# First product of two tiles by seven block products instead of eight, in rounds that take first and second product by turns

## The chip, the cores and the metric

The kernel runs on one core of one Trainium2 chip. The metric is device time in microseconds, the median of several executions. The core has four engines that compute, each with a queue of its own that it works through in order: TensorE (PE in the profile, with PEld for its weight loads), VectorE (DVE), ScalarE (ACT) and GpSimd (POOL). SyncE (SP) starts most transfers. [...]

## The reference

Attention with a threshold, then a feed-forward block. All arrays are float32 (the weights may come as 64-bit floats).

```python
batch, n_heads, seq, head_dim = (8, 8, 576, 64)
scores = q @ k.T / 8
scores = where(scores >= max(scores) - tau, scores, -1e9)
attn = exp(scores - max(scores)); attn /= sum(attn) + 1e-9
x = (attn @ v) laid out as (8 * 576, 512)         # 4608 tokens
h = x @ w_in                                      # (4608, 1024)
solu = h * softmax(h)
ln = (solu - mean) / sqrt(var + 1e-6) * g_ln
out = ln @ w_out                                  # (4608, 512)
```

## The kernel before

Attention goes by slots. A slot `(b, kind, hp, r)` holds 128 query rows of two heads against all 576 keys; a batch has 18 slots (`PER`), the kernel 144 (`NS`). The main loop runs in rounds, one slot each, and writes out by hand what every engine does in which order (`tc.manual_schedule()`); what is issued earlier in a round stands earlier in its engine's queue. A round issues, in this order:

- `begin` jobs, then `ff_norm` of a tile;
- `scores` (line 472): eight matmuls of 64x64 blocks into the two PSUM tiles `s0` and `s1`, of which there is one each, so the next round's scores wait until they are read;
- `maxes` on DVE (line 494, a scan of each head's scores that leaves the row's extreme), `ramp` on ACT (line 509, reads the scores and the extreme), `exps` on ACT (line 518, in place with row sums);
- `normalise` of the slot before on POOL (lines 525 to 528), then `middle` jobs;
- one `step` of the feed-forward block, and, where it is due, `attend_steps` (line 582, the product pv of the transposed weights `wT` with v, three rounds after its second slot) with `attended` (line 614), ACT's copy of pv into the token tile `xh` or `xe`;
- `blocks` of the slot before: two transposes on DVE (line 540); after every second slot the transposed rows are sent by SP into `wT` (lines 549 to 556);
- `late` jobs; GpSimd's scaling and gathering of coming q; a `flip` on DVE (line 212) for coming q or k; loads.

The feed-forward block works on 36 tiles of 128 tokens: 32 from `xh` (two tiles for each batch and kind), four from `xe`. Each tile takes four steps in four rounds: two halves of the first product (`ff_h`, line 647, 16 matmuls of 64x64x512 each; line 637 with whole 128x128 blocks after the last slot) and two halves of the second (`ff_o`, line 752). So two rounds with `ff_h`, and mostly pv, are followed by two with `ff_o`. Between the products stand, in jobs of later rounds: `ff_max` (DVE, 662), `ff_exp` (ACT, 671), `ff_mul` (DVE, 677), `ff_sum` (POOL, 682 and 683), `ff_stats` (DVE 692 and 693, then five small operations on POOL), `ff_norm` (ACT, 713, writes `V`), `ff_norm2` (DVE, 718, in place on `u`), `ff_swap` (four transfers from `u` into `V`), `ff_turn` (DVE, 739, writes `uT`). `ff_out` (ACT, 767) and `ff_store` end a tile.

In `ff_h` the two row halves of PE write different banks and change over between the two halves of the product; a `fence`, a memset on POOL that waits for the last matmuls, stands between (line 108). PSUM tiles for `ff_h`, `ff_o` and pv come from two tags (`p0`, `p1`) that `take` hands out and the reader gives back.

## Time and profile before

| | us |
|---|---|
| median of 3 runs | 860.36 |
| fastest, slowest | 860.07, 865.73 |
| the profiled execution | 864.95 |
| its span | 863.2 |
| PE busy (share of the span) | 817.0 (95%) |
| DVE busy | 673.5 (78%) |
| ACT busy | 572.1 (66%) |
| POOL busy | 495.1 (57%) |
| all `ff_o` matmuls, line 752 | 273.1 |
| all split `ff_h` matmuls, line 647 | 246.1 |

The span runs from the first to the last instruction of one profiled execution; the device time has 1.75 us more around it. Busy times of a group count every stretch in which one of its instructions runs; matmuls overlap their neighbours, so the groups of PE sum to more than PE's own busy time. In the profile's groups, `out<-in` names tiles, `xN` counts instructions, and one float32 matmul shows as two.

### The profile page before, as it was taken

Reading aid. Unit: us, or ns where it says so; the run is one execution under the profiler, and the core shown is the slowest. Engines: PE = TensorE matmul, PEld = TensorE weight load, DVE = VectorE, ACT = ScalarE, POOL = GpSimd, SP = SyncE. Lnnn points to the kernel's source line nnn. Section 1 sums busy time; section 2 is a strip of 40 time slices with the busy share of each in tenths; the row PEclk is TensorE's granted clock in tenths of the full one; section 3 lists DMA queues with packets and bytes.
Section 4 is the critical chain, followed back from the end, with each engine's and each line's share of the span. In section 5 each row is a group of like instructions: output and inputs, shape, how many; then the busy total and the mean of one; then the engine's idle time right before and its main releaser. Section 6 shows DMA issues by size and latency. Waiting matters only on the chain.

```text
span 863.2 us, 36114 instructions
## 1 busy us (share of the span) xinstructions
PE 817.0 (95%) x15361; PEld 634.7 (74%) x15361; DVE 673.5 (78%) x1232; ACT 572.1 (66%) x1153; POOL 495.1 (57%) x936
## 2 busy tenths in 40 slices
PE   4659789999999999999999999999999999999997
PEld 3437567777688888888788886777788888887655
DVE  4987777978788888888788887888888888787361
ACT  5876867777667767777677766767677776775121
POOL 2876756566666656565656655565666655555120
PEclk9878999999999999999999999999999999999999
DMA  9999796997878778888788787888788887555312
GB/s 288 243 254 251 185 203 162 234 248 196 224 196 219 202 196 208 220 214 198 201 202 222 198 194 192 212 222 206 183 228 229 193 196 186 154 141 140 69 38 62
DMA packets 83712, 168.54 MB, mean 195 GB/s; under 512 B 15448, under 2 KB 45152, under 8 KB 83552
## 3 DMA queue, kind: packets, MB, share of 16 engines
q1 hardware_dynamic: 82416, 164.25, 75.5%
q8 instruction: 120, 1.97, 1.0%
q10 hardware_dynamic: 1136, 2.00, 0.7%
q14 instruction: 40, 0.33, 0.1%
HBM read 46.14 MB, written 9.44 MB: 64 GB/s over the span
## 4 chain that ended last, share of the span: by engine, by line
PE 84%; DMA 6%; ACT 4%; issue 2%; DVE 2%; POOL 1%; SPq 1%; ACTq 0%; DVEq 0%
PE o_ps L752 26%; PE h_ps L647 23%; PE s_ps L472 16%; PE pv L582 15%; DMA wT<-T 4%; PE h_ps L637 3%; ACT w L509 1%; ACT w L518 1%; DMA qT<-flip 1%; DMA w<-w 1%; DVE w L494 1%; DMA k<-in_k_dram 1%; ACT qT L374 0%; PE s_ps L337 0%; POOL w L528 0%
## 5 line engine op out<-in xcount | busy, mean ns | idle before, releaser
L752 PE MATMUL o_ps<-w,uT 64*64 64x256 f32 x4608 | 273.1, 376 | 4.3 <-issue 1.9
L494 DVE CUSTOM_DVE_ANT_0 w<-s_ps,tau_t 128x576 f32<-128x576 f32 x280 | 200.0, 751 | 94.4 <-PE s_ps L472 67.0
L509 ACT ACTIVATE w<-s_ps,nth 128x576 f32<-128x576 f32 x280 | 197.0, 739 | 110.8 <-DVE nth L494 90.8
L752 PEld LDWEIGHTS o_ps<-w,uT 64*64 64x64 f32 x4608 | 221.5, 133 | 59.3 <-ACT xh L614 12.0
L528 POOL TENSOR_SCALAR w<-w,sm 128x576 f32<-128x576 f32 x288 | 221.5, 781 | 14.3
L540 DVE STREAM_TRANSPOSE T<-w 128x576 f32<-128x576 f32 x288 | 207.5, 755 | 22.0 <-POOL w L528 20.6
L647 PE MATMUL h_ps<-w,xh 64*64 64x512 f32 x1856 | 223.1, 589 | 0.7 <-issue 0.7
L518 ACT ACTIVATE w<-w,ntau 128x576 f32<-128x576 f32 x288 | 219.8, 768 | 0.0
L582 PEld LDWEIGHTS pv<-wT,v 64*64 64x64 f32 x5760 | 179.7, 137 | 37.4 <-issue 12.8
L472 PE MATMUL s_ps<-kT,qT 64*64 64x512 f32 (+1 forms) x2048 | 177.1, 413 | 14.0 <-ACT w L509 12.0
L582 PE MATMUL pv<-wT,v 64*64 64x128 f32 (+1 forms) x5760 | 179.5, 266 | 9.7 <-DMA wT<-T 7.2
L647 PEld LDWEIGHTS h_ps<-w,xh 64*64 64x64 f32 x1856 | 131.7, 133 | 65.4 <-issue 10.6
L525 POOL TENSOR_SCALAR sm<-sm 128x2 f32<-128x2 f32 x144 | 34.7, 241 | 203.7 <-ACT w L518 200.1
L526 POOL TENSOR_TENSOR sm<-sm,mone 128x2 f32<-128x2 f32 x144 | 105.8, 735 | 12.0
L472 PEld LDWEIGHTS s_ps<-kT,qT 64*64 64x64 f32 x2048 | 76.0, 136 | 21.1 <-ACT w L509 16.4
L614 ACT COPY xh<-pv 128x256 f32<-128x256 f32 x64 | 25.0, 390 | 83.3 <-PE pv L582 83.2
L713 ACT ACTIVATE V<-u,nb,rs 128x1024 f32<-128x1024 f32 x36 | 44.7, 1241 | 39.6 <-POOL nb L703 32.6
L739 DVE STREAM_TRANSPOSE uT<-V 128x1024 f32<-128x1024 f32 x36 | 44.3, 1230 | 15.2 <-DMA V<-u 14.8
L518 ACT ACTIVATION_READ_ACCUMULATOR w<-w,ntau 128x1 f32 x288 | 55.9, 194 | 0.0
L677 DVE TENSOR_TENSOR u<-h_ps,u 128x1024 f32<-128x1024 f32 x36 | 42.8, 1189 | 9.7 <-ACT u L671 9.7
L718 DVE TENSOR_SCALAR u<-u,rs,nb 128x1024 f32<-128x1024 f32 x36 | 35.5, 987 | 17.2 <-ACT V L713 17.1
L662 DVE TENSOR_REDUCE hm<-h_ps 128x1 f32<-128x1024 f32 x36 | 43.0, 1193 | 6.0 <-PE h_ps L647 3.3
(88 smaller groups left out, 562.9 us busy)
## 6 DMA issues: line engine op xcount, KB each, us to landing
wT<-T SPq DMA_DIRECT2D x160, 288.0 KB, 6.2
wT<-T SPq DMA_DIRECT2D x64, 576.0 KB, 5.5
V<-u SPq DMA_DIRECT2D x144, 64.0 KB, 3.4
out_dram<-ob SPq DMA_DIRECT2D x71, 128.0 KB, 2.5
q<-in_q_dram SPq DMA_DIRECT2D x24, 288.0 KB, 6.1
qT<-flip SPq DMA_DIRECT2D x48, 144.0 KB, 3.8
k<-in_k_dram SPq DMA_DIRECT2D x24, 288.0 KB, 5.9
kT<-flip SPq DMA_DIRECT2D x48, 144.0 KB, 4.2
```

The lines of the kernel that those rows point to most:

```text
L472: nc.tensor.matmul(out=ps[h][ROWS[y], ks], lhsT=lhsT, rhs=d["kT"][ROWS[h], ks], start=True, stop=True,)
L494: nc.vector.tensor_tensor_reduce(out=w, in0=ps[:, 0:S], in1=(zero if loose else tau_t).to_broadcast([P, S]), scale=1.0, scalar=BIG, op0=AL ...
L509: nc.scalar.activation(out=d["w"][x], in_=d["w"][x] if d["loose"] else d["ps"][x][:, 0:S], func=AF.Prelu, bias=d["nth"][x], scale=-1.0, al ...
L518: nc.scalar.activation(out=w, in_=w, func=AF.Exp, bias=ntau, scale=1.0, accum_out=sm[:, x : x + 1])
L526: nc.gpsimd.tensor_tensor(out=sm, in0=sm, in1=mone, op=ALU.pow)
L528: nc.gpsimd.tensor_scalar(out=w, in0=w, scalar1=sm[:, x : x + 1], scalar2=1.0, op0=ALU.mult, op1=ALU.mult)
L540: nc.vector.transpose(out=T[:, :, r, h, :], in_=w)
L582: nc.tensor.matmul(out=to, lhsT=d["v"][ROWS[u], (h0 + h - u) % 4 if b > 1 else h0 + h, m ^ 4 * u if m < 8 and b < 2 else m,], rhs=rhs, sta ...
L647: mm = nc.tensor.matmul(out=h[ROWS[y], f], lhsT=x[ROWS[r], c, ROWS[y]], rhs=w1_parts[ROWS[r], c, part ^ r], start=part == 0 and c == 0, st ...
L713: nc.scalar.activation(out=V, in_=u, func=AF.Identity, bias=nb, scale=rs)
L739: nc.vector.transpose(out=uT, in_=d["V"].rearrange("p y (m x) -> p m y x", x=32))
L752: nc.tensor.matmul(out=d["o"][ROWS[z], 512 * (r ^ other) : 512 * (r ^ other) + 256], lhsT=d["uT"][ROWS[r], m].rearrange("p y x -> p (y x)" ...
```

## The change

From round 30 (`START`) to the end:

- Two PSUM tiles are taken for good: `both["h"]` (two banks) for the first product, and `both["o"]`, which holds pv in columns 0 to 127 and the second product in columns 256 to 511 of each of its two banks.
- Even rounds take first product and pv, odd rounds half of a second product (`steady_round`).
- Two tiles of one batch and kind form a pair. Their first product, which has eight block products (2 tiles x 2 halves of the contraction x 2 halves of the columns), is made of seven, with sums and differences of blocks in the manner of Strassen and Winograd. Sums of the weights are made once, on GpSimd in rounds 21 to 28 (`seven_weights`); sums of the tokens per pair, on GpSimd (`sums_a`, `sums_b`). A pair takes seven phases of eight matmuls in four even rounds: two, two, two and one. Partial results are read out in between by ACT (`keep_half`) and added up by DVE, which keeps a running maximum (`add_half`).
- pv accumulates onto zeros, which DVE writes after ACT's copy (`clear`).
- `ff_norm2` goes to GpSimd.
- `xe` tiles keep eight block products (`one_h`), in two even rounds each.
- There are two token tiles `xh` where there were four, three tiles `u`, and one `ob`. q and k of the first two batches are loaded by pairs of heads (`load_pair`) where they came by four heads.

The eight rounds from a pair's first phase on are numbered r to r+7 in `new_pair`. The core of the diff:

```diff
         b, kind, hp = key
         unit = units[key]
         wT = unit["wT"]
-        unit["y"] = take("pv")
+        unit["y"] = (None, both["o"]) if "o" in both else take("pv")
         _, y = unit["y"]
         y = y.rearrange("p (u n) -> p u n", u=2)
                                 m ^ 4 * u if m < 8 and b < 2 else m,
                             ],
                             rhs=rhs,
-                            start=m == 0, stop=m == NK - 1,
+                            start=m == 0 and "o" not in both, stop=m == NK - 1,
+                            skip_group_check="o" in both,
                         )
...
-                    [P, NP, 256], F32, tag=f"xh{(2 * b + kind) % 4}", bufs=1, name="xh"
+                    [P, NP, 256], F32, tag=f"xh{kind}", bufs=1, name="xh"
...
         nc.scalar.copy(out=to, in_=y)
-        pairs_free.append(tag)
...
+        if tag:
+            pairs_free.append(tag)
+        else:
+            clear()
+    def clear():
+        nc.vector.memset(both["o"].rearrange("p (u n) -> p u n", u=2)[:, :, 0:P], 0.0)
+    both = {}
+    seven = {}
+    order_u = []
+    def new_u():
+        x = len(order_u) % 3 if "h" in both else 0
+        if "h" in both:
+            order_u.append(x)
+        return work.tile([P, DFF], F32, tag=f"u{x}", bufs=1, name="u")
+    def block(i, j, c):
+        return w1_parts[:, 2 * i + c, j]
...
+    def seven_weights(n):
+        what, c = divmod(n, 2)
+        if what < 3:
+            if n < 3:
+                to = raw_tile("k")[:, 0:512]
+            elif n < 5:
+                to = const_sums[n - 3]
+            else:
+                to = work.tile([P, 512], F32, tag="obT", bufs=1, name="sums")
+            seven[what, c] = to.rearrange("p (a x) -> p a x", x=32)
+        to, a, b, op = (
+            lambda: (seven[0, c], block(0, 1, c), block(0, 0, c), ALU.subtract),
+            lambda: (seven[1, c], block(1, 1, c), seven[0, c], ALU.subtract),
+            lambda: (seven[2, c], block(1, 0, c), seven[1, c], ALU.subtract),
+            lambda: (block(0, 1, c), block(0, 1, c), block(1, 1, c), ALU.subtract),
+        )[what]()
+        nc.gpsimd.tensor_tensor(out=to, in0=a, in1=b, op=op)
+    def sums_a(ts):
+        x1, x2 = [tokens(t) for t in ts]
+        both["s"] = work.tile([P, 2, P], F32, tag="sum", bufs=1, name="sum")
+        nc.gpsimd.tensor_tensor(out=both["s"], in0=x2[:, 0:2], in1=x2[:, 2:4], op=ALU.add)
+        nc.gpsimd.tensor_tensor(out=x2[:, 0:2], in0=x2[:, 0:2], in1=x1[:, 0:2], op=ALU.subtract)
+    def sums_b(ts):
+        x1 = tokens(ts[0])
+        nc.gpsimd.tensor_tensor(out=x1[:, 0:2], in0=both["s"], in1=x1[:, 0:2], op=ALU.subtract)
+        nc.gpsimd.tensor_tensor(out=x1[:, 2:4], in0=x1[:, 2:4], in1=x1[:, 0:2], op=ALU.subtract)
...
+    PHASES = ((1, 2), (2, 1), (6, 5), (5, 6), (7, 3), (3, 7), (4, 4))
+    def product(ts, n, c):
+        x1, x2 = [tokens(t) for t in ts]
+        return {
+            1: lambda: (x1[:, c], block(0, 0, c)),
+            2: lambda: (x1[:, 2 + c], block(1, 0, c)),
+            3: lambda: (x1[:, 2 + c], block(1, 1, c)),
+            4: lambda: (x2[:, 2 + c], seven[2, c]),
+            5: lambda: (both["s"][:, c], seven[0, c]),
+            6: lambda: (x1[:, c], seven[1, c]),
+            7: lambda: (x2[:, c], block(0, 1, c)),
+        }[n]()
+    def phase(ts, k):
+        h = both["h"]
+        last = []
+        for c in range(2):
+            for r, n in enumerate(PHASES[k]):
+                bank = r if n == 4 else n in (2, 3, 5)
+                x, w = product(ts, n, c)
+                for y in range(2):
+                    mm = nc.tensor.matmul(
+                        out=h[ROWS[y], 512 * bank : 512 * bank + 512],
+                        lhsT=x[ROWS[r], ROWS[y]], rhs=w[ROWS[r]],
+                        start=c == 0 and (n, r, k) in ((1, 0, 0), (2, 1, 0), (5, 1, 2), (4, 1, 6)),
+                        stop=c == 1 and k in (1, 3, 5, 6), skip_group_check=True,
+                    )
+                    if k in (1, 3, 5) and not last:
+                        sync(mm, both["fence"])
+                    last.append(mm)
+        if k in (0, 2, 4):
+            both["fence"] = fence(last[-4:])
...
+    def keep_half(t, g, bank):
+        nc.scalar.copy(out=half(ffn[t]["x"], g), in_=half(both["h"], bank))
+    def add_half(t, g, bank):
+        d = ffn[t]
+        m = small.tile([P, 1], F32, tag=f"hm{g}", name="hm")
+        d["m"].append(m)
+        to = half(d["x"], g)
+        nc.vector.tensor_tensor_reduce(
+            out=to, in0=half(both["h"], bank), in1=to, scale=1.0, scalar=-BIG,
+            op0=ALU.add, op1=ALU.max, accum_out=m,
+        )
...
+    def pair_exp(t):
+        d = ffn[t]
...
+        nc.vector.tensor_scalar(
+            out=nm, in0=m, scalar1=n, scalar2=-1.0, op0=ALU.max, op1=ALU.mult
+        )
+        d["u"] = new_u()
+        d["se"] = small.tile([P, 1], F32, tag="se", name="se")
+        nc.scalar.activation(
+            out=d["u"], in_=d["x"], func=AF.Exp, bias=nm, scale=1.0, accum_out=d["se"]
...
+    def pair_mul(t):
+        d = ffn[t]
+        nc.vector.tensor_tensor(out=d["u"], in0=d["x"], in1=d["u"], op=ALU.mult)
+    def new_pair(ts, r):
+        a, b = ts
+        def at(when, n, job):
+            when.setdefault(r + n, []).append(job)
+        def first():
+            for t in ts:
+                ffn[t] = dict(m=[])
+            ffn[a]["x"] = new_u()
+            keep_half(a, 0, 0)
+            add_half(a, 0, 1)
+            sums_b(ts)
+        def second():
+            ffn[b]["x"] = new_u()
+            keep_half(a, 1, 0)
+            keep_half(b, 1, 1)
+        at(late, 1, first)
+        at(late, 3, second)
+        at(late, 5, lambda: (add_half(a, 1, 1), add_half(b, 1, 0), pair_exp(a)))
+        at(late, 6, lambda: (pair_mul(a), ff_sum(a)))
+        at(middle, 7, lambda: ff_stats(a))
+        at(late, 7, lambda: (keep_half(b, 0, 1), add_half(b, 0, 0), pair_exp(b)))
+        at(begin, 8, lambda: ff_norm(a))
+        at(middle, 8, lambda: (ff_norm2(a), ff_swap(a)))
+        at(late, 8, lambda: (pair_mul(b), ff_sum(b)))
+        at(middle, 9, lambda: ff_stats(b))
+        at(late, 9, lambda: ff_turn(a, r + 9))
+        at(begin, 10, lambda: ff_norm(b))
+        at(middle, 10, lambda: (ff_norm2(b), ff_swap(b)))
+        at(late, 14 if r + 14 <= NS else 11, lambda: ff_turn(b, rnd))
+        oq.extend(ts)
...
-        nc.vector.tensor_scalar(
+        (nc.gpsimd if "h" in both else nc.vector).tensor_scalar(
             out=d["u"], in0=d["u"], scalar1=rs, scalar2=nb, op0=ALU.mult, op1=ALU.add
...
-    def ff_o(t, part):
+    def ff_o(t, ms):
         d = ffn[t]
-        other = len(t) == 3 and t[0] > 1 and t[2]
-        if part == 0:
-            d["otag"], d["o"] = take("o_ps")
-        for m in range(NC * part, NC * part + NC):
+        if ms.start == 0:
+            if "o" in both and rnd < NS:
+                d["otag"], d["o"], d["oat"] = None, both["o"], 256
+            else:
+                (d["otag"], d["o"]), d["oat"] = take("o_ps"), 0
+        for m in range(ms.start, ms.stop):
             for r in range(2):
                 for z in range(2):
+                    of = 512 * r + d["oat"]
                     nc.tensor.matmul(
-                        out=d["o"][ROWS[z], 512 * (r ^ other) : 512 * (r ^ other) + 256],
+                        out=d["o"][ROWS[z], of : of + 256],
                         lhsT=d["uT"][ROWS[r], m].rearrange("p y x -> p (y x)"),
...
-        d["ob"] = ob = work.tile([P, DM], F32, tag="ob", name="ob")
-        ob, o = [x.rearrange("p (r n) -> p r n", r=2) for x in (ob, d["o"])]
+        d["ob"] = ob = work.tile([P, DM], F32, tag="ob", bufs=1, name="ob")
+        ob = ob.rearrange("p (r n) -> p r n", r=2)
+        o = d["o"].rearrange("p (r n) -> p r n", r=2)[:, :, d["oat"] : d["oat"] + 256]
+        if len(t) == 3 and t[0] > 1 and t[2]:
+            o = o[:, ::-1]
...
-        (15, load_one, 1, "k"),
-        (16, load_one, 1, "q"),
+        (10, load_pair, 4, "k"),
+        (10, load_pair, 5, "k"),
+        (11, load_pair, 4, "q"),
+        (11, load_pair, 5, "q"),
+        (15, load_pair, 6, "k"),
+        (15, load_pair, 7, "k"),
+        (16, load_pair, 6, "q"),
+        (16, load_pair, 7, "q"),
         (17, load_v, 0, (0,)),
...
-        load_qk(0, 0)
+        load_pair(0, "q")
+        load_pair(1, "q")
+        load_pair(0, "k", nc.scalar)
+        load_pair(1, "k")
...
-        load_qk(0, 1)
+        load_pair(2, "q")
+        load_pair(2, "k")
...
+        def steady_round(due):
+            if (rnd - START) % 2:
+                o_steps(NC)
+                return
+            if not hsteps and ready and ready[0][0] <= rnd:
+                ts = ready.pop(0)[1]
+                if len(ts) == 2:
+                    new_pair(ts, rnd)
+                    sums_a(ts)
+                    for k in range(0, 7, 2):
+                        hsteps.append([lambda k=k, ts=ts: phase(ts, k)])
+                        if k < 6:
+                            hsteps[-1].append(lambda k=k, ts=ts: phase(ts, k + 1))
+                else:
+                    new_one(ts[0], rnd)
+                    sum_one(ts[0])
+                    hsteps.append([lambda t=ts[0]: None, lambda t=ts[0]: one_h(t, 0)])
+                    hsteps.append([lambda t=ts[0]: one_h(t, 1)])
+            steps = hsteps.pop(0) if hsteps else []
+            if steps[1:] or steps and rnd >= NS:
+                steps[0]()
+            if due:
+                key = pv_due.pop(0)[1]
+                for _ in attend_steps(key):
+                    pass
+                done_with(key)
+            elif rnd >= NS:
+                o_steps(NC // 2 if steps else NC)
+            if steps and rnd < NS or steps[1:]:
+                steps[-1]()
...
+            if rnd == START:
+                both["h"], both["o"] = take("h2")[1], take("ov")[1]
+                clear()
+                oq.append(prev)
+                prev = None
+                assert cur is None and quarter == 0
...
+                cur is None and quarter == 0 and ready and ready[0][0] <= rnd < START - 2
...
+                    load_pair(3, "k")
+                    load_pair(3, "q")
...
-            if quarter < 2 and cur is not None:
+            if rnd >= START:
+                steady_round(due)
...
+            if 21 <= rnd < 29:
+                seven_weights(rnd - 21)
```

## Prediction

> **What bounds the kernel now.** First the page's head: TensorE (PE) is busy 95% of the span, VectorE (DVE) 78%.
>
> ```profile
> span 863.2 us, 36114 instructions
> PE 817.0 (95%) x15361; PEld 634.7 (74%) x15361; DVE 673.5 (78%) x1232; ACT 572.1 (66%) x1153; POOL 495.1 (57%) x936
> ```
>
> Then the timeline of PE in the steady part (start us, length us, engine, line, operation).
>
> ```profile
> 401.13 1.21 PE L472 MATMUL s_ps<-kT,qT 64*64 64x64 f32 x11
> 402.01 3.77 PE L647 MATMUL h_ps<-w,xh 64*64 64x512 f32 x32
> 405.44 2.19 PE L582 MATMUL pv<-wT,v 64*64 64x128 f32 x71
> ...
> 407.50 1.21 PE L472 MATMUL s_ps<-kT,qT 64*64 64x64 f32 x11
> 408.38 3.79 PE L752 MATMUL o_ps<-w,uT 64*64 64x256 f32 x64
> 411.83 1.31 PE L472 MATMUL s_ps<-kT,qT 64*64 64x64 f32 x16
> 412.81 3.79 PE L752 MATMUL o_ps<-w,uT 64*64 64x256 f32 x64
> ```
>
> Groups follow with no gap, so I count start to start. A round with half of a first product takes 6.37 us (scores 0.88, product 3.43, pv 2.06), a round with half of a second product 4.43 (0.98 and 3.45); two and two make 21.6 per four rounds, 43.2 per eight. PE sets the pace here. How near the others are shows in one round that starts at 674.98, on all engines:
>
> ```profile
> 674.98 1.29 PE L472 MATMUL s_ps<-kT,qT 64*64 64x64 f32 x16
> 676.47 0.72 DVE L494 CUSTOM_DVE_ANT_0 w<-s_ps,tau_t 128x576 f32<-128x576 f32 x1
> ...
> 677.12 0.76 DVE L494 CUSTOM_DVE_ANT_0 w<-s_ps,tau_t 128x576 f32<-128x576 f32 x1
> 677.30 1.42 ACT L509 ACTIVATE w<-s_ps,nth 128x576 f32<-128x576 f32 x2 [1.55 <-DVE nth L494]
> ...
> 679.24 1.38 DVE L540 STREAM_TRANSPOSE T<-w 128x576 f32<-128x576 f32 x2
> ...
> 679.37 0.77 ACT L518 ACTIVATE w<-w,ntau 128x576 f32<-128x576 f32 x1
> ...
> 680.13 0.57 ACT L767 COPY ob<-o_ps 128x512 f32<-128x512 f32 x1
> ```
>
> From it: the first scan (L494) starts 1.4 us after the scores do (1.49 here); two scans take 1.38 of DVE; the ramps (L509) start 0.83 after the first scan and end at 2.25; ACT is through the exponentials (L518) at 3.66; the two transposes (L540) take 1.40. The next scores need the ramps done (they free the banks s0, s1), so an odd round of 4.43 us lets the scan be late by about 0.7 (4.43 less 1.4, 2.25 and a hand-off), an even one of 6.37 by about 2.7.
>
> **The change, part by part.** Fewer products: 14 pairs of tiles take 56 matmuls where they took 64. Eight matmuls are a quarter of the pair's eight-round share, 3.43/2 = 1.715 us, so 14 x 1.715 = 24.0 us less on PE; a cycle of eight rounds (call them e0 o1 e2 o3 e4 o5 e6 o7) takes PE 43.2 - 1.7 = 41.5, e6 holding one phase only (4.65 us). In the tail four tiles at 7.0 us (L637) become two at 6.0 and others at 6.9; its PE work is 66.3 us against 69.5.
>
> Moved between engines, per pair. From DVE go two maxima (L662, 1.19 each) and two second normalisations (L718, 0.99). To DVE come four `add_half` (the form of L494 at 512 columns: 0.61, with its read 0.65), two `hm` (0.15 to 0.41, taken 0.20) and a memset of the pv columns after each of four pv. The trace has no such memset; between the 128x64 copy (0.21) and the 128x256 copy (0.42), I take 0.35. DVE's work rises by about 0.7 us, to some 36 of 41.5. To ACT come four copies of 512 columns (L767, 0.57). To GpSimd come two normalisations (L528's 1.36 ns per column x 1024 = 1.39; bounds 0.99 by DVE's row, 2.56 by L312's 2.5 ns) and four sums of 256 columns (L312: 0.64). Its queue then holds 35 us of the cycle, counting 2.6 per round for lines 525 to 528.
>
> ```profile
> L528 POOL TENSOR_SCALAR w<-w,sm 128x576 f32<-128x576 f32 x288 | 221.5, 781 | 14.3
> L677 DVE TENSOR_TENSOR u<-h_ps,u 128x1024 f32<-128x1024 f32 x36 | 42.8, 1189 | 9.7 <-ACT u L671 9.7
> L302 DVE SCALAR_TENSOR_TENSOR em<-em 128x512 int32<-128x512 int32 x16 | 13.7, 856 | 0.0
> L312 POOL TENSOR_TENSOR w<-w,em 128x512 int32<-128x512 int32 x16 | 20.5, 1279 | 0.0
> ```
>
> **The added wait.** pv now lands in a tile that is never released, and `clear()` zeroes it. In DVE's queue the memset stands behind the scans and *ahead of the transposes*, and it waits for ACT's pv copy, which stands behind that round's ramps and exponentials. From the first scan: exponentials done 3.66, copy (L614) 0.40, two hand-offs of 0.08 (the scan's read ends at 677.21, the ramp starts at 677.30), memset 0.35, so 4.5 to 4.6; transposes to 5.9. Before, 2.8 sufficed: about 3 us of DVE lie idle in each even round. Queued behind are the transposes, the multiplications, the turns and the next scan; the next odd round's second product also waits for the memset. With the next scan due 6.37 after this one there is 0.4 us of room, and none in e0 and e6.
>
> Walk of one steady cycle, first scan to first scan:
> - e0: ACT still owes the copy, exponential and first normalisation (0.57, 1.30, 1.24) from o7, so the ramps start 1.1 late; 5.9 + 1.1 + multiplication of tile b 1.13 = 8.1.
> - o1: scans 1.38, statistics 1.45, transposes 1.40, turn 1.15, `add_half` 0.65, `flip` 0.70 = 6.7.
> - e2: `sums_b` stands in GpSimd's queue behind the chain of b's statistics (2.83 + 1.94 + 1.28 = 6.1 after o1's scan), so phase 2 starts 2.5 late on PE: 6.3.
> - o3: PE's own 4.43.
> - e4: phase 4 must wait until ACT, behind o3's exponentials, has copied both banks (3.66 + 2 x 0.57 + 0.08 = 4.9 after o3's scan; PE is there at 3.9): 6.37 + 0.9 = 7.3.
> - o5: 1.38 + 1.40 + 2 x 0.65 + 0.20 + 0.70 = 5.0.
> - e6: ramps 0.4 late behind tile a's exponential; 5.9 + 0.4 + turn 1.15 + multiplication 1.13 = 8.6, where PE has only 4.65 to do.
> - o7: 1.38 + 1.45 + 1.40 + 0.1 + 0.65 + 0.20 + 0.70 = 5.9.
>
> Sum 52.3 us, against 43.2 before and 41.5 of PE.
>
> **The sum.** Rounds 30 to 143 take 613.7 us before (scores at 175.06 to the tail at 788.78). After: 12 cycles (627.6), six rounds of the thirteenth (52.3 - 8.6 - 5.9 = 37.8), three stretches of four rounds for the `xe` tiles at half a cycle each (78.4): 744, less 8 (the first cycle has no predecessor whose statistics, turn and multiplication, 3.7, fall into it; the last 17 rounds have no `flip`, 6 x 0.7): 736, so +122. Rounds 0 to 29: loads in other pieces and eight GpSimd subtractions (1.28 each, in rounds where GpSimd is 61% busy), taken as 0 (-3 to +3). Tail: -3 if nothing waits, +10 if the last tiles' chain lies open; taken as 0. Span 863 + 122 = 985, with the 1.75 us around it 987. The profiled execution (864.95) lies 0.53% above the median of the three (860.36); so the forecast for the median is 982 us.
>
> The multiplication now has both inputs in SBUF. L302, of that kind, takes 1.67 ns per column, L677 1.16: 1.13 to 1.71 us. At the upper end two per cycle add 1.2, or about 16 us over the 13 cycles. [...]
>
> **Rivals.**
> A, faster: PE stays the bound and every new wait is covered. For it: DVE's plain work, 36 us, fits in 41.5. Against: the idle 3 us in four rounds do not fit beside it (36 + 12 = 48). Time: 863.2 - 24.8 (24.0 and 0.8 in the tail) = 838.4; for the median 836.
> B, slower by a ring alone: the transposes of one even round feed the pv of the next (two rounds on) through the wT transfer, issued in 0.6 and landing in a median of 6.2, so 7.0; then pv 2.06 and 0.35 of drain, copy 0.40, hand-offs 0.16, memset 0.35, transposes 1.40: 11.7 us per two rounds against 10.8. 57 x 0.9 = +52: 912. It decides if DVE's jobs fit into its idle time after all; the queue order speaks against that.
>
> ```profile
> wT<-T SPq DMA_DIRECT2D x160, 288.0 KB, 6.2
> ```
>
> C, no change: one stalled job per cycle gives back the 1.7 us and nothing more: 860.
>
> **How the numbers follow.** Forecast 0.76, B 0.13, A 0.07, C 0.04. The range runs from just under B (912, with 7 off for a faster landing) to the forecast with the dear multiplication and the open tail (982 + 16 + 10): 905 to 1008, leaving out A and C. Faster by over 1% (about what a measurement here can tell) 0.07, within 1% 0.04, slower 0.89.
>
> **What would show it.** Right: in the profile after, PE's share falls to near 80%; the waits list has the pv memset on the pv copy near 3 us in each even round, and scores waiting for ramps; eight rounds last about 52 us; DVE has no gap from e6 to e2 but that wait. Wrong: PE back to back at 41.5 us per eight rounds, transposes that start before the pv copy, or pv waiting for wT in every even round (B).

## The result, and the profile after

| | before | after |
|---|---|---|
| median (4 runs each, taken in turns) | 860.72 us | 1060.03 us |
| fastest, slowest | 860.07, 865.73 | 1055.29, 1061.03 |
| ratio, 95% interval | | 1.229 [1.223, 1.235] |
| profiled execution, its span | 864.95, 863.2 | 1055.29, 1053.3 |
| PE's mean granted clock | 0.981 | 0.945 |

Ratios here and below leave out runs that are over 1.5% above the fastest of their kernel; this touches only `queues_only`, two runs of four.

The change makes the kernel 23% slower; the forecast was 982 us, 14% slower. The chain of work before, then the head of the page after and its chain of work:

```profile
PE 84%; DMA 6%; ACT 4%; issue 2%; DVE 2%; POOL 1%; SPq 1%; ACTq 0%; DVEq 0%
```

```profile
span 1053.3 us, 36462 instructions
PE 866.0 (82%) x15329; PEld 558.2 (53%) x15329; DVE 658.5 (63%) x1371; ACT 597.8 (57%) x1209; POOL 584.3 (55%) x1054
...
PE 28%; DVE 18%; DMA 17%; issue 12%; ACT 11%; POOL 10%; SPq 3%; DVEq 0%; POOLq 0%; ACTq 0%
```

No engine is the bound any more. The chain changes hands all the time; PE has 28% of it where it had 84% before. PE is even busy for longer than before (866 against 817 us) with fewer matmuls: they are stretched, of which more below.

The waits of after (engine, line and tile, what it waited for; us in total, times, longest):

```profile
ACT w L503 <- DVE nth L488: 224.1, 88, 7.6
DVE ov L617 <- ACT xh L609: 204.0, 51, 6.8
...
PE ov L576 <- DMA wT<-T: 41.5, 48, 2.5
DVE ov L617 <- ACT xe L609: 40.6, 7, 8.0
...
PE h L693 <- DVE hm L739: 34.2, 24, 2.5
...
PEld ov L576 <- ACT ob L968: 30.4, 18, 4.5
...
PEld h L693 <- POOL mark L110: 27.0, 19, 3.4
```

The second and fourth lines are the wait that the prediction named: the memset of the pv columns (L617) on ACT's pv copy (L609), 4.0 us each time (5.8 at the `xe` tiles). The first line is ACT's ramps waiting for the scans, which stand behind all this in DVE's queue. The others are PE waiting for the wT transfer, for the banks of `h`, for ACT's `ob` copy and for GpSimd's mark. Two rounds of the timeline show them. First e0 of a cycle (start, length, engine, line, tiles; in brackets the idle time before and its releaser):

```profile
620.20 1.47 POOL L522 TENSOR_SCALAR w<-w,sm 128x576 f32<-128x576 f32 x2
...
624.39 0.38 ACT L609 COPY xh<-ov 128x256 f32<-128x256 f32 x1
...
624.89 0.27 DVE L617 MEMSET ov<- 128x256 f32 x1 [4.22 <-ACT xh L609]
...
625.07 1.40 DVE L534 STREAM_TRANSPOSE T<-w 128x576 f32<-128x576 f32 x2
```

The transposes' input is ready at 621.67, and they start at 625.07, because the memset stands ahead of them. Then e2 and e4 of the same cycle:

```profile
637.87 3.04 SPq L924 DMA_DIRECT2D V<-u  x4
...
638.47 1.40 DVE L534 STREAM_TRANSPOSE T<-w 128x576 f32<-128x576 f32 x2
...
641.02 0.62 SPq L543 DMA_DIRECT2D wT<-T  x1
...
649.08 0.44 PE L576 MATMUL ov<-wT,v 64*64 64x128 f32 x4 [1.44 <-DMA wT<-T]
...
649.70 3.12 PE L576 MATMUL ov<-wT,v 64*64 64x128 f32 x66 [0.18 <-DMA wT<-T]
...
653.59 0.27 DVE L617 MEMSET ov<- 128x256 f32 x1 [6.83 <-ACT xh L609]
```

The transposes end at 639.87, yet SP issues wT only at 641.02: the swap of V and u, which had waited for GpSimd's norm2, stands ahead of it. wT lands late, and pv of e4 starts 1.4 us late. It then takes 3.6 us of PE's time, not the 2.15 of e0, and most of that is not the transfer: in the middle of it PE falls to half its clock. In these two stretches (start and end, length, busy time of PE, PEld, DVE, ACT and POOL with instructions, then the clock, DMA share and rate) the granted clock goes from 1.00 to 0.50:

```profile
647.13:650.55 3.42, 1.80 (x44) 1.07 (x40) 0.00 (x0) 1.98 (x5) 1.50 (x5) 1.00 0.73 226
650.55:653.96 3.41, 3.41 (x56) 2.98 (x50) 0.37 (x2) 0.39 (x1) 1.23 (x2) 0.50 0.53 170
```

Of pv's busy time 2.5 us lie in the second stretch, so by my estimate half clock makes it about 1.25 us longer. Late and slow together make its copy late, and the memset holds DVE for 6.8 us.

The steady rounds (30 to 143), start and end, length, and what each engine was busy, with the mean clock; first before, then after:

```profile
175.10:788.80 613.70, 611.11 (x11673) 493.27 (x11665) 508.36 (x920) 426.77 (x847) 371.47 (x719) 1.00 0.79 201
```

```profile
170.70:957.20 786.50, 650.81 (x11401) 408.57 (x11398) 493.72 (x1044) 449.90 (x900) 441.42 (x817) 0.95 0.62 157
```

They take 172.8 us more. PE (the first pair of numbers after the length) idles 135.7 us in place of 2.6: +133.1. It has about 24.0 us less to do, yet is busy for 39.7 more: 63.7 us of stretching. 133.1 + 63.7 - 24.0 = 172.8. Of the stretching, I estimate 33 us as PE's clock: by the trace's record of it, 73.7 us of this part ran at half clock, PE was busy in 65.6 of them, and half of that is counted (the matmuls of 64x512 took 1.06 to 1.12 us there, 0.59 else). The other 31 us were not traced to a cause. The tail has 96.1 us against 74.4, the first thirty rounds 170.7 against 175.1.

### The profile page after: what moved, and what is told of

It is laid out like the page before. It is cut to its first block, busy times and chain, and to the rows that moved or that the text cites. A ratio compares the mean times of both kernels' runs of the same rounds, so it can differ in the third digit from the quotient of the medians.

```text
span 1053.3 us, 36462 instructions
## 1 busy us (share of the span) xinstructions
PE 866.0 (82%) x15329; PEld 558.2 (53%) x15329; DVE 658.5 (63%) x1371; ACT 597.8 (57%) x1209; POOL 584.3 (55%) x1054
## 4 chain that ended last, share of the span: by engine, by line
PE 28%; DVE 18%; DMA 17%; issue 12%; ACT 11%; POOL 10%; SPq 3%; DVEq 0%; POOLq 0%; ACTq 0%
DMA wT<-T 14%; PE h L693 8%; PE ov L576 6%; DVE T L534 5%; PE s_ps L466 5%; DVE w L488 4%; PE o_ps L950 3%; ACT w L503 3%; ACT w L512 3%; DVE bs L887 3%; PE h_ps L843 2%; POOL w L522 2%; ACT V L908 2%; PE h L717 2%; DVE u L759 2%
## 5 line engine op out<-in xcount | busy, mean ns | idle before, releaser
L576 PE MATMUL ov<-wT,v 64*64 64x128 f32 (+1 forms) x4752 | 163.1, 285 | 62.4 <-DMA wT<-T 41.5
L950 PE MATMUL ov<-w,uT 64*64 64x256 f32 x3456 | 201.0, 377 | 10.1 <-DVE uT L934 10.1
L576 PEld LDWEIGHTS ov<-wT,v 64*64 64x64 f32 x4752 | 147.5, 151 | 111.2 <-issue 34.2
L950 PEld LDWEIGHTS ov<-w,uT 64*64 64x64 f32 x3456 | 142.8, 133 | 80.5 <-issue 35.6
L617 DVE MEMSET ov<- 128x256 f32 x60 | 16.3, 272 | 250.1 <-ACT xh L609 204.0
L693 PE MATMUL h<-w,xh 64*64 64x512 f32 x896 | 115.1, 616 | 36.5 <-POOL mark L110 20.5
L693 PEld LDWEIGHTS h<-w,xh 64*64 64x64 f32 x896 | 38.6, 137 | 89.6 <-issue 24.7
L950 PE MATMUL o_ps<-w,uT 64*64 64x256 f32 x1152 | 70.4, 384 | 12.4 <-DVE uT L934 8.8
L950 PEld LDWEIGHTS o_ps<-w,uT 64*64 64x64 f32 x1152 | 51.6, 136 | 33.3 <-issue 16.5
L693 PE MATMUL h<-sums,xh 64*64 64x512 f32 x336 | 63.5, 643 | 0.4 <-DVE hm L739 0.4
L693 PE MATMUL h<-k,sum 64*64 64x512 f32 x224 | 58.8, 646 | 2.1 <-POOL mark L110 2.0
```

What stands on the lines that cost most here:

```text
L576: nc.tensor.matmul(out=to, lhsT=d["v"][ROWS[u], (h0 + h - u) % 4 if b > 1 else h0 + h, m ^ 4 * u if m < 8 and b < 2 else m,], rhs=rhs, sta ...
L693: mm = nc.tensor.matmul(out=h[ROWS[y], 512 * bank : 512 * bank + 512], lhsT=x[ROWS[r], ROWS[y]], rhs=w[ROWS[r]], start=c == 0 and (n, r, k ...
L950: nc.tensor.matmul(out=d["o"][ROWS[z], of : of + 256], lhsT=d["uT"][ROWS[r], m].rearrange("p y x -> p (y x)"), rhs=w2[ROWS[r], m ^ r, 256 ...
```

## The experiments

All in comparison with the kernel before on the same chip; medians of four runs (ten for `before_norm2`), the ratio with its 95% interval. Line numbers of edited kernels are shifted by up to three.

### Where the memset stands

Theory: the memset's place in DVE's queue is the main cause. Rivals: the ring of transposes, wT, pv and copy sets the pace whatever the order (B); or the wait only fills time that DVE would idle anyway.

**The changed kernel, memset behind the transposes:**

```diff
         if tag:
             pairs_free.append(tag)
         else:
-            clear()
+            both["dirty"] = True
...
             if rnd - 1 in live:
                 blocks(rnd - 1)
+            if both.pop("dirty", False):
+                clear()
```

> The changed kernel, with the one edit that the memset of the pv columns is issued behind the round's two transposes in VectorE's queue, not ahead of them. If the queue order is the main cause (theory), transposes start about 3 us earlier in each even round; my walk of a cycle without that wait gives 3.7 us less per eight rounds, 14 cycles, so about 52 us less: near 1008 us (990 to 1025). If the ring of transposes, wT transfer, pv and copy sets the pace (rival B), the wait only moves to pv on PE and the time stays above 1040. If nothing but this wait is in the way, PE is the bound again and the time comes down to 840-860.

998.5 us, ratio 1.156 [1.148, 1.164]: 61.5 us less than after, a little more than expected. The order costs what the walk said, and it is not all: 135 us are left.

**The kernel before, with the memset alone,** behind ACT's copy in `attended`, ahead of the transposes:

```diff
         tag, y = units.pop(key)["y"]
+        units_y = y
...
         nc.scalar.copy(out=to, in_=y)
+        if rnd >= 30:
+            nc.vector.memset(units_y.rearrange("p (u n) -> p u n", u=2)[:, :, 0:P], 0.0)
         pairs_free.append(tag)
```

> The kernel before, with one addition: from round 30 on VectorE zeroes the pv columns behind ACT's pv copy and ahead of the round's transposes (no other part of the change). Theory: VectorE idles some 2.9 us and works 0.27 us more in each even round, and its work of about 8.4 us per two rounds no longer fits into 10.8: at least 0.8 us per two rounds, 57 times, +45 us: 900 to 930 us. If the wait is harmless by itself and hurts only in company of the seven products' jobs, it stays under 870 us.

960.9 us, ratio 1.115 [1.107, 1.123]: +98, twice what was expected. Nearly all of the change is absent here, and a loss half as large as its own (98 against 199 us) is there. The trace shows a chain that I had not walked:

```profile
511.40 0.39 ACT L615 COPY xh<-pv 128x256 f32<-128x256 f32 x1
...
511.92 0.27 DVE L617 MEMSET pv<- 128x256 f32 x1 [2.79 <-ACT xh L615]
512.10 1.40 DVE L540 STREAM_TRANSPOSE T<-w 128x576 f32<-128x576 f32 x2
...
513.43 1.20 DVE L742 STREAM_TRANSPOSE uT<-V 128x1024 f32<-128x1024 f32 x1
...
514.78 5.37 PE L755 MATMUL o_ps<-w,uT 64*64 64x256 f32 x64 [2.45 <-DVE uT L742]
```

Memset, transposes, turn, second product: the turn stands behind the transposes, and PE waits 2.45 us for it. The first of every two `ff_o` rounds mostly takes 7.1 or 8.8 us in place of 4.43: 2.7 to 4.4 us more, once in four rounds, 28 times, is 76 to 123 us. The rounds of 8.8 are those with a stretch of half clock in them: ten stretches of 3.41 us, PE busy throughout, which, counted at half as above, make 17 of the 98 us (the 5.37 us of the last line above, for matmuls that took 3.79 before, are one of them). DVE is busy for 71% of the span, less than before; it was never full.

**The same memset behind the transposes** (the tag given back after it):

> The kernel before with the same added memset, issued behind the round's transposes instead of ahead of them. Ahead of them it made 961 us of 863. If its place in VectorE's queue is the cause (theory): the transposes are 3 us earlier, wT and turn with them; what is left is the wait that still stands ahead of the turn and the multiplications, some 10 to 35 us: 870 to 900. If a wait for pv's copy anywhere in VectorE's queue costs the same: 940 or more.

901.8 us, ratio 1.045 [1.041, 1.049]. Of the 98 us, 59 are the place ahead of the transposes, with what follows from it, the half clock too, which does not occur in these rounds here. 38 stay: the memset still stands ahead of the turn, for which PE waits 29.2 us in all, against 62.8 with the memset ahead of the transposes and none in the kernel before.

**The changed kernel, zeroing on ACT, no memset on DVE:**

```diff
         else:
-            clear()
+            nc.scalar.mul(both["o"].rearrange("p (u n) -> p u n", u=2)[:, :, 0:P], both["o"].rearrange("p (u n) -> p u n", u=2)[:, :, 0:P], 0.0)
```

> The changed kernel with one edit: ACT zeroes the pv columns behind its own copy, VectorE has no memset. The changed kernel's 250 us of VectorE's waiting before the memset are gone. With the memset behind the transposes it took 998. If the order was all that counted: 990 to 1005. If the 128 us of waiting that were left there still cost: 960 to 985. Rival, the memset's wait was only filling VectorE's idle time: over 1040.

1010.3 us, ratio 1.173 [1.166, 1.180]: no better than the memset behind the transposes. So 50 to 62 us of after's loss come from the memset's wait ahead of the transposes. In the changed kernel with the memset behind them DVE still waits 128 us for pv; taking these away too gains nothing that shows. How much of them ACT's own zeroing (0.37 us each time, 21.7 in all) eats up again was not separated.

### GpSimd's normalisation

One part alone, on the kernel before, and the same part undone in the changed kernel (the engine of `ff_norm2`):

```diff
-        nc.vector.tensor_scalar(
+        (nc.gpsimd if 30 <= rnd < NS else nc.vector).tensor_scalar(
```

> The kernel before, with one addition: in rounds 30 to 143 u's second normalisation runs on GpSimd (no other part of the change). Theory: VectorE loses 1.0 us per tile that was not on the path, GpSimd gains 1.2 us per tile at 57% busy: within 5 us of 860. Rival: standing in GpSimd's queue it delays the swap of V and u, or the next scores' normalisation, and the time goes up by 10 us or more.

> The changed kernel, with the one edit that u's second normalisation is back on VectorE. Theory: GpSimd is not the cause; VectorE, whose queue is on the path, gets 1.0 us more per tile and the swap comes a little earlier: 1045 to 1080 us. Rival: GpSimd's queue is the bound (late swaps keep wT waiting in SP's queue, late marks keep the phases waiting): the time falls by 20 us or more, to 1040 or less.

864.0 us, ratio 1.002 [0.998, 1.005], and 1060.2 us, ratio 1.227 [1.219, 1.235]. Where u is normalised makes no difference that can be told from the runs' spread, in either direction.

### Queues, marks and sums

Two queues in another order, with the memset where it is:

```diff
-   begin.setdefault(rnd + 1, []).append(lambda: ff_out(t, last))
+   begin.setdefault(rnd + 1, []).insert(0, lambda: ff_out(t, last))
...
-        at(middle, 8, lambda: (ff_norm2(a), ff_swap(a)))
+        at(middle, 8, lambda: ff_norm2(a))
+        late.setdefault(r + 8, []).insert(0, lambda: ff_swap(a))
...
```

Tile b alike.

> The changed kernel with the memset left where it is, and two queues put in another order: ACT copies the second product's result (ob) ahead of V's normalisation at the start of a round, and SP issues the swap of V and u behind the wT transfers of the round. If the excess of the cycles over my walk (54.95 against 52.3 us, and the longer xe quartets) is the late wT and the pv that waits for ob, some 25 to 40 us go: 1020 to 1035. If the memset's order hides these waits (they only fill time that VectorE loses anyway), it stays above 1045.

1109.4 us (1094.8 to 1112.0), ratio 1.275 [1.264, 1.287]: by the ratios some 40 us slower than after. The rival (above 1045) holds, but that it would be slower neither side had expected. The trace of one odd and the next even round:

```profile
655.47 3.33 SPq L926 DMA_DIRECT2D V<-u  x4
...
660.66 1.25 DVE L936 STREAM_TRANSPOSE uT<-V 128x1024 f32<-128x1024 f32 x1 [3.55 <-DMA V<-u]
661.83 0.65 DVE L739 CUSTOM_DVE_ANT_0 u<-h,u 128x512 f32<-128x512 f32 x1
...
662.65 1.12 PE L693 MATMUL h<-k,xh 64*64 64x512 f32 x2 [5.43 <-DVE hm L739]
```

The swap now waits for wT, which waits for transposes, which wait for the memset. The turn then waits 3.55 us for the swap, `add_half` stands behind the turn, and PE's next phase waits 5.43 for the bank of `h`. The prompter wT was paid for by a later swap.

The same two orders with the memset behind, then GpSimd's and ACT's jobs moved as well (norm2 and `sums_a` behind the marks, `sums_b` and `second` at the start of their rounds), then ACT's zeroing in place of the memset:

> The changed kernel with the memset behind the transposes and the two queues in the other order (ob copy first on ACT, swap behind wT on SP). In the run with the memset behind, pv still waited 63 us in all for ob and 22 for wT. If these are on the path: 998 less 25 to 50, 950 to 975 us. If the next wait takes their place (GpSimd's marks and sums, 75 us of PE's waiting), it stays above 985.

> As the run before it in this job (memset behind the transposes, ob copy first, swap behind wT), and GpSimd's and ACT's jobs moved too: norm2 and the first sums behind the phases' marks, the second sums at the start of the next round ahead of the statistics' chain, the copies of both banks ahead of the ramps of their round. By the waits that PE shows there (1.6 us for the mark, 1.8 for the second sums, 0.4 to 1.3 for the bank copies, each once in eight rounds, 14 cycles) another 50 us go: 900 to 930. If VectorE's plain order of jobs is what is left, it stays above 945; if only these waits were in the way, PE is the bound again, 840 to 860.

> The same, but ACT zeroes the pv columns right behind its own copy (a multiplication by 0 in place of VectorE's memset). VectorE then waits for nothing of pv's at all. If that wait, 128 us in the run with the memset behind, still costs: 15 to 35 us below the run before it; if it lies in VectorE's idle time: within 8 us of it, ACT having 0.4 us more in each even round.

983.3 us (1.139 [1.133, 1.146]), 982.7 (1.139 [1.133, 1.145]) and 980.5 (1.134 [1.127, 1.141]). The orders give 15 us; the other two steps nothing. Most rounds of the last run take PE's own time, but all that is late meets in one (a late cycle): 7.4, 4.4, 13.2, 4.4, 6.4, 4.4, 6.5, 4.4 us from e0 to o7. There phase 2 waits 3.8 us for `add_half`.

### The one h tile

The phases have a single tile of two banks, so each must wait until the one before it is read out. These runs empty the banks earlier: ACT's copies ahead of the ramps, `add_half` right behind the scans.

```diff
-        at(late, 1, first)
-        at(late, 3, second)
...
+        at(begin, 1, first)
+        middle.setdefault(r + 1, []).insert(0, lambda: add_half(a, 0, 1))
+        at(begin, 3, second)
...
```

Rounds 5 and 7 alike. In the first two runs `first` still holds GpSimd's `sums_b`, which so comes earlier too; in the others it was there already.

> The changed kernel, memset where it is; only the copies and sums that empty the two banks of h come earlier in their rounds: ACT's copies ahead of the ramps, VectorE's add_half right behind the scans (not behind transposes and turn). The phases have one h tile, so the next phase waits for these. Theory: the memset's order still sets the cycle, and the phases only wait in time that VectorE loses anyway: 1035 to 1070 us. Rival, the phases' wait for the one h tile is the larger cost: under 1010.

> The same, and the memset behind the transposes. The run with the memset behind alone takes 998 us. If the single h tile is what is left of the loss: 950 or less; if not, 985 or more. Each phase that no longer waits 2 us once or twice in eight rounds makes 14 x 2 to 4 = 28 to 56 us.

> ACT zeroes the pv columns, both queue orders and GpSimd's jobs moved as in the run with all of these (980 us), and the banks of h emptied early. There, a third round of each cycle takes 11 to 13 us where 6.4 would do, because a phase waits 4 us for add_half behind VectorE's turn, which waits for the late swap. Theory (single h tile): 14 x 4 to 6.5 us go, 890 to 925. Rival, the late swap and turn themselves: above 955.

> As the run before it, but SP issues the swap ahead of the round's wT transfers again (norm2 stays behind the phases' marks on GpSimd). If the late swap is what holds VectorE's turn: 10 to 30 us below the run before it; if the late wT is worse: 10 to 30 above; if the single h tile was all: within 8.

1061.9 us (1.230 [1.225, 1.235]), 1011.2 (1.175 [1.168, 1.183]), 954.5 (1.107 [1.102, 1.113]) and 994.4 (1.152 [1.148, 1.157]). Alone the edit does nothing; with the memset behind it even costs 13; on top of all other edits it gives 26. So the late emptying is one of several waits, and not the larger cost by itself; no run gave the phases a second tile. SP's order alone is worth 40 us between the last two: here the swap behind wT is the better place, where in `queues_only` (with `ob` moved too) it was the worse.

### GpSimd's load

The 954 us run still has one round of 9 to 13 us in each eight, where a phase waits for GpSimd's mark. These two runs take work off GpSimd (norm2 and the four sums; norm2 alone):

> As the run of 954 us (ACT clears, banks emptied early, ob first), but u's second normalisation and the pair's four sums run on VectorE, the normalisation and the swap at their places of before (swap ahead of wT). In the 954 run one round in eight still takes 9 to 13 us, because GpSimd is busy from the chain of the statistics to the mark without a gap, and a phase waits 3 us for the mark. If GpSimd's load is what is left: 14 x 3 to 5 us less, 890 to 915. If VectorE's queue takes over: 940 or more.

> The same with the four sums left on GpSimd; only the normalisation is VectorE's. If GpSimd's normalisation (1.19 us) ahead of marks and sums is the larger part: within 12 us of the run before it; if the sums are (2.9 us per pair): 15 to 35 us above it.

963.8 us (1.116 [1.112, 1.121]) and 959.1 (1.110 [1.104, 1.117]). Neither gains on 954.5, but this does not refute the theory, because each run changes two things: the swap is ahead of wT again, the order that cost 40 us above. Against the run of 994.4 us, which has that order too, they gain 31 and 35 us; all of it comes with the normalisation, none with the sums. PE's wait for the mark falls from 28.2 us (run of 954.5) to 13.6 and 15.0, and pv's for wT rises from 20.4 to 32.2 and 32.9. The normalisation on DVE with the swap behind wT was not run.

### Seven or eight products, and a later pv

```diff
-                ts = ready.pop(0)[1]
+                at_, ts = ready.pop(0)
                 if len(ts) == 2:
+                    ready.insert(0, (at_, ts[1:]))
+                    ts = ts[:1]
+                if len(ts) == 2:
```

> The changed kernel with one part undone: in rounds 30 to the end no pair is made of seven products; each tile of a pair gets its own first product (eight block products per pair, 64 matmuls), in the way the xe tiles have it in the changed kernel. By turns, one h tile, memset ahead of the transposes and GpSimd's norm2 stay. PE has 24 us more to do. If the memset's place sets the cycle whatever the product is (theory): within 40 us of 1060. If the phases' own waits (bank copies, add_half, marks, sums) make the excess over my walk: under 1000. By the xe quartets of the changed kernel, 30.2 us against 27.5 for half a cycle, it would be slower: 28 x 2.7 = 75 more, near 1135.

1023.6 us, ratio 1.186 [1.177, 1.196]: with 24 us more for PE to do, 36 us less than after. That is within the theory's 40 us, at its edge. The seven products with all that comes with them (sums, marks, read-outs of both banks) cost about 60 us here: 36, and the 24 they were to save. My extrapolation from the `xe` quartets was wrong: where no pair precedes or follows, four rounds take some 25 us.

```diff
-            pv_due.append((s + LAG_PV + (
+            pv_due.append((s + LAG_PV + 2 * (s + LAG_PV >= START) + (
```

> As the run of 954 us (ACT clears, banks emptied early, queues moved), but from round 30 on each pv comes two rounds later, so the wT transfer has two rounds more to land (the same two wT buffers). If the late wT transfers are what is left: pv waits for no wT, 905 to 935 us. If it is GpSimd's marks, ob and the phases: within 10 us of 954. If the buffers, held longer, make the transfer wait for pv in their place: 965 or more.

944.7 us, ratio 1.095 [1.088, 1.101]: the best form of the change tried, and still 80 us behind the kernel before. pv no longer waits for wT in the steady rounds, which gives 10 us, no more. In the cycle shown, seven rounds of eight take 4.4 to 6.9 us; e2 takes 9.6, and GpSimd's queue shows why:

```profile
617.70 1.47 POOL L522 TENSOR_SCALAR w<-w,sm 128x576 f32<-128x576 f32 x2
...
622.30 1.47 POOL L522 TENSOR_SCALAR w<-w,sm 128x576 f32<-128x576 f32 x2
...
623.71 0.10 POOL L110 MEMSET mark<- 128x1 f32 x1
...
623.86 0.65 PE L693 MATMUL h<-k,sum 64*64 64x512 f32 x2 [3.00 <-POOL mark L110]
```

Two slots' normalisations, with a tile's chain of statistics between them, stand ahead of a mark of 0.1 us, and PE stands still for it. And e6, with one phase only, takes 6.5 us though PE has 4.65 to do: pv waits 1.6 for the `ob` copy, which stands behind tile a's exponential on ACT.

## Why the prediction was right or wrong

**Right: the sign and the memset's wait.** The memset stands ahead of the transposes and waits for ACT's pv copy. DVE idles 4.0 us for it, 51 times (about 3 predicted), and taking it out of the way gives 50 to 62 us; the walk with and without it differs by 3.7 us per cycle, 52 in all. PE's share fell to 82% ("near 80%"), and neither rival A (836) nor C (860) came about. The signs were mixed: eight rounds last 55 us, not 52, and pv waits for wT in 27 of the 57 even rounds, where the sign of B was every one.

**Right: most rounds of the walk, in this cycle.** Scan to scan from 619.23 on: 8.3, 6.6, 6.7, 4.4, 10.8, 4.7, 8.1 us from e0 to e6, with 5.2 for the o7 before it; the walk had 8.1, 6.7, 6.3, 4.4, 7.3, 5.0, 8.6, 5.9. Other cycles have their long round elsewhere.

**Wrong: the step from the walk to the steady part.** The prediction has 736 us for rounds 30 to 143; they took 786.5. Three terms:
- The cycle, 52.3 us: the twelve measure 54.95 on average, +31.8. In the cycle shown the excess is e4's, 10.8 us for 7.3. I had put the ring of transposes, wT, pv and copy down as rival B, *instead of* the queue order, and so left it out of the forecast; in fact both act at once, the late wT making the memset's wait longer (the second timeline above). And the walk has PE at full speed in every round, while a stretch of half clock lies in this e4.
- The three `xe` quartets, "half a cycle each (78.4)": 29.2, 30.5 and 30.8, +12. In the last two pv waits 3.7 us for the `ob` copy, since both share one tile and ACT has the copy behind V's normalisation; in the first it waits 2.0 us for wT. Half clock follows in all three. No step of mine had these waits.
- "Less 8" for the first cycle and the last rounds: it did not appear, +8.

**Wrong: the tail,** taken as 0 (-3 to +10): +21.7. About 10 of it goes away with the memset (86.1 us where ACT zeroes). Half clock, counted at half as above, makes about 5 (1.6 where ACT zeroes), so the two overlap; what makes the rest was not tested.

**Wrong: the step from span to median.** I took the profiled run of before, 0.53% above its median, as the rule; after's lies 0.45% below its own. That is 10 of the 78 us missed (the others: 50.5 + 21.7, less 4.4 in the early rounds).

**Wrong in the range.** It ended at the forecast with a dear multiplication and an open tail. It should have held the forecast *and* the ring together.

**Sums that do not come out.** B's ring has issue and landing at 7.0 where its terms, 0.6 and 6.2, make 6.8; with these B is near 901, not 912. DVE's work was to rise by 0.7 us per cycle; the terms given make less than 0.1, and it fell (508.4 to 493.7 us in the steady rounds). Neither changes the forecast of 982; the first would have put the lower end of the range near 894.

**A cost that no step held: PE's clock.** The trace's record of the granted clock knows two values here, 1.00 and 0.50, and changes only at multiples of 3.41 us. The kernel before has no half clock in its steady rounds, after has 73.7 us of it. By the estimate above it costs PE 33 us, two thirds of the 50.5 that the steady part was missed by. How much of the 33 was on the path was not separated.

In these traces the length of a gap tells less of what comes after it than how busy PE was within one such stretch. In the run of 944.7 us a gap of 3.00 fell across two stretches, and the clock stayed; here is the second of them:

```profile
622.14:625.55 3.41, 1.69 (x16) 0.67 (x20) 2.98 (x7) 3.39 (x6) 2.74 (x5) 1.00 0.39 87
```

In the run of 954.5 us a gap of 3.06 fell into one, and the clock of the next was halved:

```profile
581.02 1.12 PE L693 MATMUL h<-k,sum 64*64 64x512 f32 x2 [3.06 <-POOL mark L110]
```

```profile
577.33:580.74 3.41, 0.64 (x24) 0.39 (x16) 3.40 (x7) 2.39 (x3) 2.97 (x7) 1.00 0.16 36
580.74:584.15 3.41, 3.13 (x16) 1.05 (x20) 1.00 (x2) 2.43 (x7) 3.14 (x7) 0.50 0.99 250
```

The first product's matmuls took 0.60 to 0.65 us behind the gap of 3.00, and 1.06 to 1.12 behind that of 3.06. In the steady rounds of after, all ten full-clock stretches with PE busy for less than 40% were followed by half clock, seven of the 18 with 40 to 55%, and none of the 181 with more. In e4 above a gap of 1.44 us was enough, with PE busy for 1.80 of 3.42. So in these steady rounds waits that filled half of such a stretch or more mostly (16 times of 21) cost PE twice: while they lasted, and in the matmuls behind them.

**The prices.** Memset 0.27 (0.35 taken), norm2 on GpSimd 1.19 (1.39), the sums 0.73 (0.64), the multiplication with both inputs in SBUF 1.195 (1.13 to 1.71):

```profile
L913 POOL TENSOR_SCALAR u<-u,rs,nb 128x1024 f32<-128x1024 f32 x32 | 38.1, 1190 | 13.9 <-ACT V L908 13.1
...
L759 DVE TENSOR_TENSOR u<-u 128x1024 f32<-128x1024 f32 x28 | 33.5, 1195 | 2.7 <-ACT u L753 2.7
```

The last is 6 ns from the form that read one input from PSUM before (1189). None of these prices decided anything.

On GpSimd's side the trace of after shows an instruction that ran beside this multiplication and took longer:

```profile
626.36 1.31 POOL L519 TENSOR_SCALAR sm<-sm 128x2 f32<-128x2 f32 x1
626.40 1.18 DVE L759 TENSOR_TENSOR u<-u 128x1024 f32<-128x1024 f32 x1
```

The same GpSimd instruction takes 0.23 us elsewhere (at 619.08). Eleven of GpSimd's instructions beside this multiplication are longer in this way, by 0.4 to 1.1 us and 8 us in all. What makes them longer, and whether any of it was on the path, was not tested.

**What stays open.** With every wait that I found moved, the change still costs 80 us. Eight products instead of seven take away 36 us from the kernel as changed; I did not run both together, nor the rounds by turns without the shared tile for pv and second product. How the 80 divide between the single `h` tile, the shared `ov` tile, GpSimd's marks and PE's clock (some 14 us even in the steady rounds of the best run) is therefore not settled.

## What to carry to other kernels

A wait is priced by the queue behind it: a memset of 0.27 us in each even round cost 98 us in a kernel that had 22% of DVE free, because the transposes and the turn stood behind it and PE waited for the turn. Rings that are each near the limit can act together, as they did here, so add a second ring to the forecast and don't keep it as an alternative to the first. And before work is saved on the bound engine, count what the saving brings with it: here sums, marks and read-outs between the phases, which took back the 24 us saved and 36 more. Whether the single PSUM tile makes them so dear was not tested: the run with eight products has it too. Last, where the bound engine starts to wait, look at its clock before you call a long group of matmuls late data.

## What the runs showed of the hardware

- PE's clock: in the trace of after, stretches of half clock are 3.41 us long or a multiple, and in its steady rounds they follow a stretch of full clock in which PE was busy for about half or less (all ten with PE busy for under 40%, seven of 18 with 40 to 55%, none of 181 with more). Matmuls of 64x512 took 0.59 to 0.65 us at full clock and 1.06 to 1.12 at half.
- GpSimd's `tensor_scalar` on 1024 columns takes 1.19 us (after) where DVE's took 0.99 (before), both on average; which of the two makes it changed the whole time by 0.2% or less in either kernel (`before_norm2`: ratio 1.002; `norm2_dve`: 1.227 against after's 1.229).
- A GpSimd instruction beside a DVE multiplication with both inputs in SBUF took up to 1.31 us in place of 0.23 (after, at 626.36 us); eleven in all were longer, by 0.4 to 1.1 us each.
- PE's busy time rose (817 to 866 us) with fewer matmuls: by the estimate above, 33 us of the steady part's stretching are half clock. One pv whose `wT` landed piece by piece added less: at full clock, that of 702.33 (after) was busy for 2.6 us in place of 2.15, over 3.6 us.
